# Two layers of attention and gated units on one core: half of the second layer's attention products as three f16 rounds instead of one f32 product

## The chip, the cores and the metric

The kernel runs on one core of a Trainium2 chip. The metric is the device time of one execution in microseconds, as the median of several runs. The engines are named as the profile names them: PE (TensorE) does the matrix products, ACT (ScalarE) and DVE (VectorE) the work on rows, POOL (GpSimd) the rest of it, and SP (SyncE) issues most of the DMAs.

## The reference

The computation applies the same attention block and the same gated block twice, with the same weights, to a sequence of 2048 rows of 448 numbers. There are 16 query heads of 28 numbers and one key head and one value head that all of them share.

```python
def _A_ref(x, wq, wk, wv, wo):
    q = (x @ wq).reshape(B, S, H, Dh).transpose(0, 2, 1, 3)
    k = x @ wk
    v = x @ wv
    scores = einsum("bhqd,bkd->bhqk", q, k) * (Dh ** -0.5)
    p = softmax(scores, axis=-1)
    o = einsum("bhqk,bkd->bhqd", p, v)
    return o.transpose(0, 2, 1, 3).reshape(B, S, H * Dh) @ wo

def _B_ref(x, w_gate, w_up, w_down):
    h = sigmoid(x @ w_gate) * (x @ w_up)
    return h @ w_down

x = x + _A_ref(layernorm(x), wq, wk, wv, wo)
x = x + _B_ref(layernorm(x), w_gate, w_up, w_down)
x = x + _A_ref(layernorm(x), wq, wk, wv, wo)
x = x + _B_ref(layernorm(x), w_gate, w_up, w_down)
```

## The kernel before

The kernel issues its instructions in an order written out by hand (`manual_schedule`), and each engine works through its own instructions in that order.

A layer (`l` is 0 or 1) is cut into 16 units (`u`) of 128 query rows, and a unit into 16 steps (`kt`) of 128 keys. In a step, `scores` is called four times, once for each group `g` of four heads. It makes one f16 product `s` of 128 keys by 512 (four heads times 128 rows), and ACT turns it into the probabilities `P` (128x512, f32, not yet divided by their sum) with an exponential. The scores are made in one f16 product although more than f16 precision is kept: the operand has the high part of the keys, the low part and the row maximum side by side in its 96 rows.

`pv` multiplies the values `VV` (128 keys by 32 columns: 28 values, a column of ones that gives the sum of the probabilities, and zeros) with the four `P` of a step, in f32. The four products of a step go side by side into four column tiles of 32 (`tile_position=(0, 32 * g)`) and add up over the 16 steps of a unit in one PSUM bank.

The order of work inside a step is a string in `PATHS`. A letter S is one call of `scores`, P one call of `pv` on the oldest step that waits, M one group of row maxima for a later unit (four `mx` products, then four reductions on DVE), X one tick of the work on finished units (`tile`, stages `f0` to `ff`), and F one slice of filling work (the gated block, `wo`, queries). Two strings alternate over even and odd steps. For the second layer from unit 4 they are

```python
"D0": ("FXFFSSSSPPM", "FSFSFXSFFMS"),     # even units up to 12
"D1": ("SFFXFSFSSPPM", "SFSFFFXSFSFM"),   # odd units up to 13
"E0": ("FXFFSSSSPPM", "SSFFFXSFFMS"),     # unit 14
"E1": ("SFSFXFSSFPPM", "SSSFFXSM"),       # unit 15
```

So the two P of a pair stand together in the even step: first the product of the even step before, then that of the odd step before. Between a score and its use lie a whole pair for an even step and one step for an odd one.

Work that follows a product is put off with `defer(fn, lag)`; `flush()` issues what has come due, at the start of each slice and whenever a PSUM tile is taken for filling work, and `flush(True)` issues everything that is pending, due or not. Seven PSUM banks (tag `f`) are shared by the scores, the maxima and the filling work; `P` has 14 buffers.

The stages of a finished unit that matter here: `f0` to `fw` send the sums through DRAM and back as `lb`; `fa` (step 7) multiplies on POOL (L671); `fb` (step 8) casts the result on ACT (L677) and takes the remainder on DVE (L678); `wo_products` follows, and its end starts the statistics of the layer norm with six small POOL instructions (L308 to L313); `fd` (step 14) does the norm on DVE and the remainder `hl` on POOL (L324, L325). In the gated block, `glu` leaves `ev` (DVE, L756), then `parts` (ACT, L759) with a lag of 3 and the remainder of `h` (DVE, L760) with another lag of 3.

Of the kernel before, what the change touches and what calls it, by code (L numbers as in the profile page):

```python
# [8 lines left out]
F32 = mybir.dt.float32  # L9
F16 = mybir.dt.float16  # L10
I32 = mybir.dt.int32
AF = mybir.ActivationFunctionType
OP = mybir.AluOpType
# [6 lines left out]
def interleaved_layers_kernel(ctx: ExitStack, tc: tile.TileContext, x, wq, wk, wv, wo, wg, wu, wd, out, layers=2):  # L20
# [6 lines left out]
    nc = tc.nc  # L27
    _, S, D = x.shape
    F = wg.shape[1]
    H, Dh = 16, 28  # L30
    NT, NB, G, KT, FC = S // 128, S // 512, H // 4, S // 128, F // 128
# [6 lines left out]
    cst = ctx.enter_context(tc.tile_pool(name="cst", bufs=1))  # L38
    drm = ctx.enter_context(tc.tile_pool(name="drm", bufs=1, space=DRAM))
    big = ctx.enter_context(tc.tile_pool(name="big", bufs=5))  # L40
    lay = ctx.enter_context(tc.tile_pool(name="lay", bufs=2))
    wk1 = ctx.enter_context(tc.tile_pool(name="wk1", bufs=2))
# [23 lines left out]
    def defer(fn, lag=0):  # L66

        pend.append((now[0] + lag, fn))

    def flush(every=False):  # L70
        todo, pend[:] = pend[:], []
        for i, (due, fn) in enumerate(todo):
            if due > now[0] and not every:
                pend.append((due, fn))
            else:
                fn()
        if every and pend:
            flush(True)

    def fps(shape, dt, name):  # L80
        flush()
        return psf.tile(shape, dt, tag="f", name=name, bufs=NBK["f"])
# [13 lines left out]
    pwb = cst.tile([128, 4], F32, name="pwb")  # L96
    swb = cst.tile([128, 4], F32, name="swb")
    esc = cst.tile([128, 1], F32, name="esc")
    gsc = cst.tile([128, 1], F32, name="gsc")
    osc = cst.tile([128, 1], F32, name="osc")  # L100
    dsc = cst.tile([128, 1], F32, name="dsc")
# [260 lines left out]
    for t in ktl:  # L362
        nc.vector.memset(t, 0.0)
        nc.vector.memset(t[:, 0, 28:29], 32768.0)
    KK, VV, QH = {}, {}, {}

    def layer_tiles(l):
        KK[l] = lay.tile([128, 2, S], F16, tag="KK", name="KK")
        VV[l] = lay.tile([128, KT, 32], F32, tag="VV", name="VV")
        nc.vector.memset(VV[l][:, :, 28:32], 0.0)  # L370
        nc.vector.memset(VV[l][:, :, 28:29], 1.0)

    def kv(l, XT, t, kt):

        p = fps([128, 56], F32, "kv")
        yield from chain(p, lambda a, c, k: WKV[:k, a, c], lambda c, k: XT[:k, c, t * 128:(t + 1) * 128], 40, False)
        kt_ = ktl[kt % 2]

        def build():
            k = p[:, 0:28].rearrange("p (o d) -> p o d", o=1).to_broadcast([128, 7, 28])  # L380
            nc.scalar.activation(kt_[:, 1:8, 0:28], k, AF.Copy, scale=2.0 ** -18)
            nc.scalar.activation(VV[l][:, kt, 0:28], p[:, 28:56], AF.Copy, scale=2.0 ** -16)
            nc.vector.scalar_tensor_tensor(kt_[:, 0, 0:28], p[:, 0:28], 2.0 ** -18, kt_[:, 1, 0:28],
                                           op0=OP.mult, op1=OP.subtract)
        defer(build)
# [49 lines left out]
    QS, QH, PVS = {}, {}, {}  # L435
# [147 lines left out]
    def scores(l, u, kt, g, P):  # L583
        assert ("m", l, u) in stored, (l, u, kt)
        s = psf.tile([128, 512], F32, tag=BANKS["s"], name="s", bufs=NBK[BANKS["s"]])
        nc.tensor.matmul(s, KK[l][0:96, 0, kt * 128:(kt + 1) * 128], QS[l, u][:, g].rearrange("p h n -> p (h n)"),  # L586
                         start=True, stop=True)
        p = wk1.tile([128, 512], F32, tag="P", name="P", bufs=14)
        nc.scalar.activation(p, s, AF.Exp, scale=esc)  # L589
        P.append(p)  # L590

    def pv(l, u, kt, P):
        if kt == 0:
            PVS[l, u] = psv.tile([128, 512], F32, tag="v", name="pv")
        v = PVS[l, u]
        for g in range(4):
            nc.tensor.matmul(v[32 * g:32 * g + 32], VV[l][:, kt], P[g], start=kt == 0, stop=kt == KT - 1,  # L597
                             tile_position=(0, 32 * g))
        if kt == KT - 1:
            o = wk1.tile([128, 512], F32, name="pvs", bufs=1)  # L600
            nc.scalar.copy(o, v)
            PVS[l, u] = o
# [285 lines left out]


    layer_tiles(0)  # L890
    XT0 = [big.tile([128, 7, 512], F16, tag="big", name="XT0") for _ in range(NB)]
    QH0 = wk1.tile([128, G, 512], F16, tag="wgu", name="QH0", bufs=WB)
    for b in range(NB):
        XTQ[0, b] = XT0[b]
    xr0 = {}

    def load_x0(i, eng=nc.sync):
        if i < HB:
            xr0[i] = wk1.tile([128, D], F32, tag="h", name="xr0", bufs=HB)
        else:  # L900
            xr0[i] = wk1.tile([128, D], F32, tag="P", name="xr0", bufs=14)
        eng.dma_start(xr0[i], x[0, i * 128:(i + 1) * 128])

    hl0, ls0 = {}, {}
# [126 lines left out]
    for o in SEQ.split():  # L1031
        a = o.split(",")
# [35 lines left out]
    for l in range(layers):  # L1068
# [8 lines left out]
        else:  # L1077
            mx.todo.sort()
            n = sum(a[0] < 4 for a in mx.todo) + 4
# [10 lines left out]
        for step in range(U * KT):  # L1090
            u, kt = divmod(step, KT)
            if step == HEAD and not final:
                mxs[l + 1] = Maxima(l + 1)
            P = []
            pair = pair_of(l, u)
            single = len(pair) == 2 and "P" in pair[0] and "P" in pair[1]
            for o in pair[kt % len(pair)]:
                if o == "S":
                    scores(l, u, kt, len(P), P)
                elif o == "M":  # L1100
                    if l and step < 3 * KT:
                        n = step in sparse
                    else:
                        n = 1 + (u == 0 and kt in MORE)
                    if not n:
                        mx.visit()
                    for _ in range(n):
                        if not mx.step() and not final and l + 1 in mxs:
                            a = mxs[l + 1].between()
# [24 lines left out]
        while waiting:  # L1134
            pv(*waiting.pop(0))
        flush(True)
        later(*BLK[l, NBL - 1].tile(U - 1))
        n = 0
        nx = None if final else mxs[l + 1]
        while side or pend or (fill.gens if final else not nx.started()):  # L1140
# [4 lines left out]
            a = None if final else nx.between()  # L1145
            if a:
# [7 lines left out]
                if go:  # L1154
                    nx.step(a)
                    n = 0
# [25 lines left out]
```

## Time and profile before

| | us |
|---|---|
| Median of three runs | 2247.08 (2245.97 to 2248.66) |
| Span of the profiled execution | 2242.6 |
| Busy PE / DVE / ACT / POOL in the span | 2197.5 / 1633.7 / 1556.5 / 328.6 |
| Second layer, units 4 to 15, by the copies of their sums | from 1410 to 2157 |
| An even unit / an odd unit there | 64 / 62 |

The profiled execution is not timed apart from its span; the median of the runs is 4.5 us above the span, and these 4.5 us are taken as what lies around it. A product on PE is listed with a duration that runs from its entry into the array to its end, so neighbours overlap; the distance from start to start tells what one costs. Rows of the timeline give the start, the busy time, the engine, the line, what is written and read, and how many instructions were merged into the row. The bracket at the end is the idle time before it and what ended that.

### The profile page before, as it was taken

The page shows a single profiled execution, that of the slowest core. Times are in us where ns is not written, and L with a number is a line of the kernel's source. Part 1 is how long each engine was busy: PE and PEld are TensorE (multiplying, and loading weights), DVE is VectorE, ACT ScalarE, POOL GpSimd, SP SyncE. Part 2 cuts the span into 40 slices and gives each one's busy share as a digit, 9 for nine tenths or more (in the row PEclk, how much of TensorE's full clock was granted, in tenths as well). Part 3 has the DMA queues.
Part 4 walks back from the last instruction along what each step waited for, and adds up shares of the span by engine and source line. Part 5 has one row for each costly group of instructions (what it writes and reads, how often), then busy time and mean ns, then how long its engine had stood idle before and what let it go on. Part 6 is the DMA issues. An engine that isn't in the chain of part 4 may idle for free.

```text
span 2242.6 us, 41405 instructions
## 1 busy us (share of the span) xinstructions
PE 2197.5 (98%) x15922; PEld 1032.1 (46%) x15922; DVE 1633.7 (73%) x2902; ACT 1556.5 (69%) x2603; POOL 328.6 (15%) x567
## 2 busy tenths in 40 slices
PE   7899999999999999999999999999999999999999
PEld 3322344444444444454564334445454545445457
DVE  7888887778778777777796557777777777777222
ACT  5698887777667677676514997777676767777741
POOL 4123764001110100101011010000000000000010
PEclk9999999999999999999999999999999999999999
DMA  5232662324323132422441123232231313132333
GB/s 174 70 98 87 209 211 83 105 62 118 98 67 102 58 109 61 127 78 69 135 136 40 31 56 113 52 107 80 86 101 58 107 50 104 56 107 78 97 105 118
DMA packets 203622, 213.28 MB, mean 95 GB/s; under 512 B 135376, under 2 KB 164240, under 8 KB 203424
## 3 DMA queue, kind: packets, MB, share of 16 engines
q1 hardware_dynamic: 198880, 195.88, 29.6%
q0 software_dynamic: 4544, 14.77, 1.7%
q8 instruction: 124, 2.03, 0.4%
q14 instruction: 74, 0.61, 0.1%
HBM read 175.37 MB, written 23.59 MB: 89 GB/s over the span
## 4 chain that ended last, share of the span: by engine, by line
PE 86%; DVE 4%; DMA 2%; ACT 2%; issue 1%; SPq 1%; POOL 0%; ACTq 0%; POOLq 0%; DVEq 0%
PE pv L597 20%; PE s L586 20%; PE dn L786 11%; PE gp L354 11%; PE up L354 11%; PE mx L551 7%; PE wo L697 3%; DVE mp L556 3%; PE qp L354 2%; ACT P L589 1%; DMA rc<-sums 1%; DMA sums<-rc 0%; DMA rgu<-in_B_w_gate_dram 0%; DMA lb<-sums 0%; PE hot L918 0%
## 5 line engine op out<-in xcount | busy, mean ns | idle before, releaser
L589 ACT ACTIVATE P<-s,esc 128x512 f32<-128x512 f32 x2048 | 1295.7, 692 | 455.8 <-PE s L586 444.6
L556 DVE TENSOR_REDUCE mp<-mx 128x1 f32<-128x512 f32 x2048 | 1269.6, 683 | 387.1 <-PE mx L551 382.7
L586 PE MATMUL s<-QS,KK 96*128 96x512 f16 x2048 | 687.0, 382 | 13.3 <-DVE mp L556 9.0
L354 PEld LDWEIGHTS <-wgu 128*128 128x128 f16 x4928 | 470.6, 97 | 174.6 <-issue 30.1
L597 PE MATMUL pv<-P,VV 128*32 128x512 f32 x4096 | 510.3, 602 | 0.0
L354 PE MATMUL gp<-XT,wgu 128*128 128x256 f16 x2464 | 350.3, 272 | 0.8 <-DVE mp L556 0.8
L354 PE MATMUL up<-XT,wgu 128*128 128x256 f16 x2464 | 347.7, 272 | 0.0
L786 PE MATMUL dn<-WD,h 128*128 128x448 f16 x1344 | 299.9, 352 | 0.0
L586 PEld LDWEIGHTS <-KK 96*128 96x128 f16 x2048 | 190.7, 97 | 232.6 <-issue 142.2
L597 PEld LDWEIGHTS pv<-P,VV 128*32 128x32 f32 x4096 | 98.7, 108 | 240.1 <-issue 238.9
L551 PE MATMUL mx<-KK,QH 32*128 32x512 f16 x1792 | 186.8, 384 | 5.3 <-DVE mp L556 1.9
L786 PEld LDWEIGHTS <-h 128*128 128x128 f16 x1344 | 127.1, 97 | 127.6 <-issue 11.2
L551 PEld LDWEIGHTS <-QH 32*128 32x128 f16 x1792 | 46.5, 91 | 247.8 <-issue 245.4
L671 POOL TENSOR_TENSOR lb<-pvs,lb 128x512 f32<-128x512 f32 x32 | 41.2, 1287 | 622.3 <-DMA lb<-sums 548.7
L759 ACT ACTIVATE h<-th 128x512 f16<-128x512 f32 x112 | 70.4, 628 | 67.4 <-DVE th L756 67.3
L308 POOL TENSOR_SCALAR rs<-mv 128x1 f32<-128x1 f32 (+1 forms) x50 | 12.2, 244 | 678.0 <-DVE mv L293 676.0
L354 PE MATMUL qp<-XT,WQ 128*128 128x512 f16 x352 | 109.5, 389 | 1.0 <-DVE mp L556 0.7
L756 DVE SCALAR_TENSOR_TENSOR th<-th,up 128x512 f32<-128x512 f32 x112 | 76.2, 680 | 42.2 <-PE up L354 36.7
L748 ACT ACTIVATE th<-gp,gsc 128x512 f32<-128x512 f32 x112 | 76.8, 686 | 32.3 <-PE gp L354 32.2
L760 DVE SCALAR_TENSOR_TENSOR h<-th,h 128x512 f16<-128x512 f32 x112 | 77.0, 688 | 29.6 <-ACT h L759 29.6
L697 PE MATMUL wo<-WO,oT 128*128 128x448 f16 x384 | 88.8, 352 | 0.9 <-ACT oT L677 0.5
L354 PEld LDWEIGHTS <-WQ 128*128 128x128 f16 x352 | 33.6, 99 | 49.7 <-issue 23.1
(158 smaller groups left out, 908.2 us busy)
## 6 DMA issues: line engine op xcount, KB each, us to landing
wgu<-wgu_d SPq DMA_DIRECT2D x224, 512.0 KB
QS<-qd SPq DMA_DIRECT2D x384, 32.0 KB
lb<-sums SPq DMA_DIRECT2D x128, 64.0 KB
xr<-in_A_x_dram SPq DMA_DIRECT2D x32, 224.0 KB
qd<-qst POOLq DMA_DIRECT2D x28, 256.0 KB, 2.6
wgu_d<-sgu POOLq DMA_DIRECT2D x14, 512.0 KB, 4.0
x2d<-x SPq DMA_DIRECT2D x16, 224.0 KB
xr<-x2d SPq DMA_DIRECT2D x16, 224.0 KB
```

The lines of the kernel that those rows point to most:

```text
L354: nc.tensor.matmul(ps, a, b, start=n == 0, stop=n == 10)
L551: nc.tensor.matmul(ps[h][:, i * w:(i + 1) * w], qh[32 * h:32 * h + 32, g], KK[l][32 * h:32 * h + 32, 1, ka:kz], start=True, stop=True, til ...
L556: nc.vector.tensor_reduce(o, ps[h].rearrange("p (g k) -> p g k", g=n), axis=AX.X, op=OP.max)
L586: nc.tensor.matmul(s, KK[l][0:96, 0, kt * 128:(kt + 1) * 128], QS[l, u][:, g].rearrange("p h n -> p (h n)"), start=True, stop=True)
L589: nc.scalar.activation(p, s, AF.Exp, scale=esc)
L597: nc.tensor.matmul(v[32 * g:32 * g + 32], VV[l][:, kt], P[g], start=kt == 0, stop=kt == KT - 1, tile_position=(0, 32 * g))
L697: nc.tensor.matmul(p, v["oT"][:, a, h * 128:(h + 1) * 128], WO[:, c, h], start=n == 0, stop=n == 11)
L748: defer(lambda: nc.scalar.activation(th, gp.rearrange("p j n -> p (j n)"), AF.Tanh, scale=gsc))
L756: nc.vector.scalar_tensor_tensor(t, th, 1.0, up.rearrange("p j n -> p (j n)"), op0=OP.add, op1=OP.mult)
L759: nc.scalar.activation(h[:, 0], t, AF.Copy, scale=2.0 ** -17)
L760: defer(lambda: nc.vector.scalar_tensor_tensor(h[:, 1], t, 2.0 ** -17, h[:, 0], op0=OP.mult, op1=OP.subtract), 3)
L786: nc.tensor.matmul(p, hs[f // 2][:, a, o:o + 128], WD[:, f, c], start=n == 0, stop=n == 3 * FC - 1)
```

## The change

In the second layer the exponential gets a bias of 4 ln 2, which multiplies every probability and their sums by 16. From unit 4 of that layer on, the probabilities of every even step are split: a high part `hi` in f16 (a copy, by DVE for groups 0 and 2 and by ACT for groups 1 and 3) and a remainder `lo` in f16 (a subtraction on POOL). The split is put off with a lag of 3 slices. The values are split in the same way into `VH`, on POOL, when they are made. `pv` of such a step is then twelve f16 products in three rounds of four column tiles, high by high, low values by high, high values by low, after a `flush(True)`. The parts lie three groups to a tile in the pool `big`. `P` has 13 buffers instead of 14.

```diff
+    up4 = cst.tile([128, 1], F32, name="up4")
+    nc.vector.memset(up4, 4 * math.log(2))
...
     def layer_tiles(l):
...
+        if l:
+            VH[l] = lay.tile([128, KT, 2, 32], F16, tag="VH", name="VH", bufs=1)
...
             nc.scalar.activation(VV[l][:, kt, 0:28], p[:, 28:56], AF.Copy, scale=2.0 ** -16)
+            if l in VH:
+                nc.gpsimd.tensor_copy(VH[l][:, kt, 0], VV[l][:, kt])
+                nc.gpsimd.tensor_tensor(VH[l][:, kt, 1], VV[l][:, kt], VH[l][:, kt, 0], op=OP.subtract)
...
-        p = wk1.tile([128, 512], F32, tag="P", name="P", bufs=14)
-        nc.scalar.activation(p, s, AF.Exp, scale=esc)
-        P.append(p)
+        p = wk1.tile([128, 512], F32, tag="P", name="P", bufs=13)
+        nc.scalar.activation(p, s, AF.Exp, scale=esc, bias=up4 if l else 0.0)
+        if not halved(l, u, kt):
+            P.append(p)
+            return
+        if not hold or hold[1] == 3:
+            hold[:] = [big.tile([128, 7, 512], F16, tag="big", name="PH"), 0]
+        t, n = hold
+        hold[1] += 1
+        hi, lo = t[:, 2 * n], t[:, 2 * n + 1]
+        P.append((hi, lo))
+        how = HI[g]
+
+        def part():
+            if how == "a":
+                nc.scalar.copy(hi, p)
+            else:
+                (nc.vector if how == "d" else nc.gpsimd).tensor_copy(hi, p)
+            nc.gpsimd.tensor_tensor(lo, p, hi, op=OP.subtract)
+        defer(part, HLAG)
+
+    hold = []
+    HI, HLAG = "dada", 3
+
+    def halved(l, u, k):
+        return l and u > 3 and k % 2 == 0
 
     def pv(l, u, kt, P):
...
         v = PVS[l, u]
-        for g in range(4):
-            nc.tensor.matmul(v[32 * g:32 * g + 32], VV[l][:, kt], P[g], start=kt == 0, stop=kt == KT - 1,
-                             tile_position=(0, 32 * g))
+        if halved(l, u, kt):
+            flush(True)
+            for n, (a, c) in enumerate(((0, 0), (1, 0), (0, 1))):
+                for g in range(4):
+                    nc.tensor.matmul(v[32 * g:32 * g + 32], VH[l][:, kt, a], P[g][c],
+                                     start=kt == 0 and n == 0, stop=kt == KT - 1 and n == 2,
+                                     tile_position=(0, 32 * g))
+        else:
+            for g in range(4):
+                nc.tensor.matmul(v[32 * g:32 * g + 32], VV[l][:, kt], P[g], start=kt == 0, stop=kt == KT - 1,
+                                 tile_position=(0, 32 * g))
...
-            xr0[i] = wk1.tile([128, D], F32, tag="P", name="xr0", bufs=14)
+            xr0[i] = wk1.tile([128, D], F32, tag="P", name="xr0", bufs=13)
```

More of the change, by code (lines that the diff above doesn't have):

```diff
@@ L364, in interleaved_layers_kernel @@
         nc.vector.memset(t[:, 0, 28:29], 32768.0)
-    KK, VV, QH = {}, {}, {}
+    KK, VV, VH, QH = {}, {}, {}, {}
     def layer_tiles(l):
```

## The prediction

> **What bounds the kernel now.** I read the page first, then the busy times by unit, the waits of the second layer, and the timeline of one even and one odd unit.
>
> ```profile
> span 2242.6 us, 41405 instructions
> PE 2197.5 (98%) x15922; PEld 1032.1 (46%) x15922; DVE 1633.7 (73%) x2902; ACT 1556.5 (69%) x2603; POOL 328.6 (15%) x567
> 1663.00:1727.00 64.00, 64.00 (x452) 28.89 (x448) 47.47 (x81) 44.57 (x71) 4.01 (x9) 1.00 0.20 58
> 1727.00:1789.00 62.00, 61.65 (x482) 31.57 (x478) 48.73 (x83) 46.40 (x75) 4.01 (x9) 1.00 0.40 110
> 2105.00:2157.00 52.00, 52.00 (x393) 28.32 (x392) 8.78 (x15) 40.66 (x70) 4.03 (x9) 1.00 0.38 119
> ACT P L589 <- PE s L586: 162.7, 232, 1.5
> DVE mp L556 <- PE mx L551: 126.4, 127, 2.2
> PE s L586 <- DVE mp L556: 0.6, 2, 0.3
> ```
>
> The three long rows are unit 8 (even), unit 9 (odd) and unit 15: length, then busy PE, weight loads, DVE, ACT, POOL, and the granted clock (1.00). The last three are waits between 1474 and 2105 us (units 5 to 14). PE is never idle there, and the others wait for it: ACT 163 us of 631 for scores, DVE 126 us for maxima, PE only 0.6 us for DVE. So a shorter product shortens these units, as long as what is added to ACT, DVE and POOL fits where they wait.
>
> **The product.** One even and one odd unit, a pair of steps each, PE first, then ACT, then DVE:
>
> ```profile
> 1699.23 1.05 PE L586 MATMUL s<-QS,KK 96*128 96x512 f16 x4
> 1700.21 1.92 PE L597 MATMUL pv<-P,VV 128*32 128x512 f32 x16
> 1702.06 0.39 PE L551 MATMUL mx<-KK,QH 32*128 32x512 f16 x4
> 1708.45 1.92 PE L597 MATMUL pv<-P,VV 128*32 128x512 f32 x16
> 1716.99 1.85 PE pv L597 x16
> ...
> 1706.18 0.69 ACT L589 ACTIVATE P<-s,esc 128x512 f32<-128x512 f32 x1 [0.85 <-PE s L586]
> 1707.91 2.42 ACT L589 ACTIVATE P<-s,esc 128x512 f32<-128x512 f32 x4 [1.04 <-PE s L586]
> 1711.67 0.69 ACT L589 ACTIVATE P<-s,esc 128x512 f32<-128x512 f32 x1 [1.33 <-PE s L586]
> ...
> 1705.85 2.48 DVE L556 TENSOR_REDUCE mp<-mx 128x1 f32<-128x512 f32 x4 [0.88 <-PE mx L551]
> 1710.77 1.89 DVE L556 TENSOR_REDUCE mp<-mx 128x1 f32<-128x512 f32 x3
> ...
> 1764.17 1.92 PE L597 MATMUL pv<-P,VV 128*32 128x512 f32 x16
> 1771.36 1.06 PE L597 MATMUL pv<-P,VV 128*32 128x512 f32 x8
> 1763.90 1.84 ACT L589 ACTIVATE P<-s,esc 128x512 f32<-128x512 f32 x3 [0.73 <-PE s L586]
> 1766.78 2.63 ACT L589 ACTIVATE P<-s,esc 128x512 f32<-128x512 f32 x4 [1.03 <-PE s L586]
> 1762.16 2.48 DVE L556 TENSOR_REDUCE mp<-mx 128x1 f32<-128x512 f32 x4 [0.78 <-PE mx L551]
> 1766.45 2.48 DVE L556 TENSOR_REDUCE mp<-mx 128x1 f32<-128x512 f32 x4 [0.34 <-PE mx L551]
> ```
>
> Two `pv` take 1702.06 - 1700.21 = 1.85 us from start to start, one 0.93: sixteen products are four rounds of four column tiles, 0.46 each, two to a step, because an f32 product is listed as two. Four f16 products of 512 columns in a row (1699.23) start (1.05 - 0.38) / 3 = 0.22 apart, 0.38 being the duration of one. If four column tiles run beside each other in f16 as they do in f32, a round costs 0.22, three 0.66, and a halved step saves 0.27 us. There are 12 units x 8 = 96 of them: 25.9 us, the whole the change can give.
>
> The low end of that price comes from the only packed f16 product, the four `mx`, whose successor starts 0.32 later:
>
> ```profile
> 1603.53 0.40 PE L551 MATMUL mx<-KK,QH 32*128 32x512 f16 x4
> 1603.85 0.39 PE L586 MATMUL s<-QS,KK 96*128 96x512 f16 x1
> 1605.81 0.16 PEld L597 LDWEIGHTS pv<-P,VV 128*32 128x32 f32 x8 [0.42 <-issue]
> 1606.27 0.13 PEld L597 LDWEIGHTS pv<-P,VV 128*32 128x32 f32 x4 [0.30 <-issue]
> ```
>
> Three times 0.32 is 0.96, dearer than f32 by 0.03. I take 0.22: the 0.32 holds a change of tiling on leaving, which inside three equal rounds does not occur, and eight weight loads stand at the start of the f32 rounds, so those of the second round are loaded ahead. Four loads take 0.13, which fits under 0.21.
>
> The Trainium skill (TensorE: Matmul & The Clock Gate, Part 3, what overlaps) says that a weight load runs under a product only if its row group differs. All four column tiles here use all rows, so by that rule the loads would stand open. The loads at 1605.81 go against it. By that rule a round would be 0.22 + 0.13 = 0.35, three 1.05, and the kernel slower by 96 x 0.12 = 11.5 us, to 2259.
>
> **What is added.** Four groups per pair, with durations from the group rows:
>
> ```profile
> L323 DVE CAST hl<-xn 128x448 f16<-128x448 f32 x10 | 3.9, 394 | 0.3
> L677 ACT CAST oT<-lb 128x512 f16<-128x512 f32 x10 | 6.1, 607 | 0.0
> L143 POOL TENSOR_TENSOR sgu<-rgu,sgu 128x512 f16<-128x512 f32 x9 | 10.4, 1160 | 0.7
> L760 DVE SCALAR_TENSOR_TENSOR h<-th,h 128x512 f16<-128x512 f32 x35 | 23.6, 674 | 0.0
> 230.30 1.16 POOL L143 TENSOR_TENSOR sgu<-rgu,sgu 128x512 f16<-128x512 f32 x1
> 230.39 1.62 DVE L131 SCALAR_TENSOR_TENSOR sgu<-rgu,swb,sgu 128x512 f16<-128x512 f32 x1
> ```
>
> DVE: two copies of 0.394 x 512 / 448 = 0.45, so 0.90. ACT: two of 0.61, so 1.22. POOL: four of 1.16, and about 0.09 between them (estimate), so 5.0 of a pair of about 8 us. POOL was idle for 60 of 64 us.
>
> Where they fall: `part` has a lag of 3 slices, but each halved `pv` calls `flush(True)` and so issues the parts of its own step at once, just ahead of the two `pv`. In unit 8 that is 1708.45. Exponentials end there at 1708.5, 1709.1, 1709.7, 1710.3. Between 1708.33 and 1710.77 DVE has nothing but, once a unit, a row maximum (two `pv` make this gap in every pair), so it copies group 0 at once; POOL's first remainder runs to about 1710.3. The copy of group 2 is ready at 1709.8 and meets it.
>
> The last two rows show what then happens: a DVE instruction that reads two tiles in SBUF began 0.09 after a POOL subtraction, ended when that had ended plus 0.55, and was listed with 1.62, where a like one (L760) takes 0.67. So the second copy waits about 0.5 and ends at 1710.75; the next maxima, which a shorter `pv` brings to about 1710.5, are delayed by 0.25, and the gap of 0.88 ahead of the following ones takes that up.
>
> The Trainium skill (SBUF — State Buffer, on the pair of ports shared by VectorE and GpSimd) says the same: one holds the pair for a whole instruction, the other blocks fully, and copies and casts can be of the holding kind. By that rule every copy may lose 1.16 to a remainder; rival three prices this.
>
> ACT's two copies follow the exponentials at 1710.33 and end at 1711.6, in the gap of 1.33. The remainders of groups 1 to 3 follow, the last ending near 1714.8, 6.3 after the `pv` that issued it. It is needed in the third round of the next pair, 1716.99 + 0.44: 2.6 us to spare. So even units keep the whole: 6 x 8 x 0.27 = 13.0 us.
>
> An odd unit has less room. DVE is idle 62 - 48.73 = 13.3 us. Copies take 8 x 0.90 = 7.2, waits of the second copy 8 x 0.5 = 4.0, and the remainders of `h`, four in such a unit, meet a busy POOL (8 x 4.64 / 62 = 0.6 of the time) for half an instruction: 4 x 0.6 x 0.58 = 1.4. That leaves 0.7 of the 2.2 us wanted; I take 0.5: 5 x 0.5 = 2.5 us. In unit 15 ACT is idle 52 - 40.66 = 11.3, and 16 x 0.61 = 9.8 leaves 1.5; I take 1.0.
>
> Losses. POOL's two jobs for a finished unit now stand in line:
>
> ```profile
> 1747.81 1.27 POOL L671 TENSOR_TENSOR lb<-pvs,lb 128x512 f32<-128x512 f32 x1 [28.90 <-DMA lb<-sums]
> 1755.65 0.61 ACT L677 CAST oT<-lb 128x512 f16<-128x512 f32 x1
> 1766.20 0.22 POOL L308 TENSOR_SCALAR rs<-mv 128x1 f32<-128x1 f32 x1 [17.12 <-DVE mv L293]
> 1767.98 0.19 POOL L313 TENSOR_TENSOR rs<-rs 128x1 f32<-128x1 f32 x1
> 2150.63 1.92 PE L597 MATMUL pv<-P,VV 128*32 128x512 f32 x16
> 2154.77 1.92 PE L597 MATMUL pv<-P,VV 128*32 128x512 f32 x16
> ```
>
> The product `lb` runs 6.6 us ahead of the ACT cast that needs it. Behind four remainders it would end some 7 us later than now, so the cast, with the exponentials behind it, starts about 0.6 late; half is absorbed by ACT's gaps: 5 x 0.3 = 1.5 us in odd units, nothing in even ones with their longer steps. The six `rs` instructions hold POOL for 2.0 us, between the first and second remainder of a pair: in unit 9 the last remainder then ends near 1772.4 and is wanted at 1771.36 + 0.44; 0.6 x 5 = 3.0 us. In unit 4 the first halved step has no halved `pv` beside it and waits its lag: 1 us (estimate). At the end the last halved `pv` (2154.77) comes 4.1 after the one that issues its parts; the remainder needs 6.3, the third round is at 4.6: 1.7 us.
>
> At nothing: the 32 small POOL instructions for `VH` (POOL idles), the bias (ACT's input beside the scale, same shape), and the thirteenth buffer (twelve `P` are in flight at most when two `pv` release eight, and the scores of the fourteenth stand behind these `pv` on PE anyway). The early issue of pending work by `flush(True)` brings ACT's `h` and its DVE remainder forward into the same gap; the work is the same, so zero, between -3 and +5.
>
> Sum: 13.0 + 2.5 + 1.0 - 1.5 - 3.0 - 1.0 - 1.7 = 9.3 us. The span goes to 2233.3, and with the 4.5 us around it the time to 2238.
>
> **Rivals.** *All of it is kept* (odd units hide the additions too): 25.9 - 2.7 for the two single losses, 2224. For it: waits of DVE for maxima are 126 us in ten units, copies need 72. Against it: the 0.34 left ahead of the maxima at 1766.45.
>
> *The product does not get shorter*: a round costs 0.32, nothing is saved, and the losses of 7 us stand partly in the shadow: 2247, from 2243 to 2255.
>
> *The shared reads decide against it* (slower): both DVE copies of a pair wait for a remainder, 1.62 - 0.67 = 0.95 each. An odd pair then needs 48.73 / 8 + 0.90 + 1.9 = 8.9 on DVE instead of 7.75, an even one 47.47 / 8 + 2.8 = 8.7 instead of 8.0. Then 40 odd pairs give +46 and 40 even ones +28: 2321 at worst. With one full wait per pair it is 7.95 against 7.75 in odd pairs, +8, and even ones still fit: about 2245. It decides from about 0.75 us of waiting per odd pair, where DVE has no idle time left; halfway, 2275. For it: the 1.62. Against it: at the time of the first copy POOL has been through for 2 us.
>
> **How the numbers follow.** This measurement can tell about 0.2% (4.5 us) from no change. Chances: forecast (2230 to 2243) 0.44, all kept (2221 to 2230) 0.18, no shorter product 0.16, shared reads 0.17 (2250 to 2321), loads that stand open 0.05. Below 2242.6: 0.44 + 0.18, less 0.01 for the forecast's edge, 0.61; within: this 0.01, 0.13 of the third and 0.02 of the fourth, 0.16; above 2251.6: the other 0.03, 0.15 and 0.05, 0.23. The range reaches from 2222 to 2262; what is left out is the top of the second case (0.04) and the worse half of the fourth (0.12). The likeliest case alone is 2230 to 2243.
>
> **What would show it.** Halved `pv` as twelve f16 products in about 0.66 us; DVE casts at 0.45 for group 0 and near 1 for group 2; remainders at 1.16; even units near 62 us, odd ones near 61.5; PE's idle time in units 5 to 14 a few us and ended by POOL. Rounds 0.3 apart, DVE busy over 95% of an odd unit, or waits of PE for POOL in every pair would make it wrong.

## Result and profile after

The changed kernel takes 2278.8 us (median of four, 2276.8 to 2280.4) against 2247.9: a ratio of 1.014 (95% interval 1.0126 to 1.0155), slower by 31 us. 2238 had been forecast, with a range up to 2262.

The page of the changed kernel: span, busy times, then groups (line, engine, what is written and read, count, busy us, mean ns, idle before):

```profile
span 2276.6 us, 43034 instructions
PE 2200.2 (97%) x16306; PEld 1043.5 (46%) x16306; DVE 1739.7 (76%) x3095; ACT 1724.7 (76%) x2795; POOL 787.4 (35%) x983
L596 ACT ACTIVATE P<-s,esc 128x512 f32<-128x512 f32 x1024 | 650.2, 691 | 235.0 <-PE s L593 228.9
L596 ACT ACTIVATE P<-s,up,esc 128x512 f32<-128x512 f32 x1024 | 729.6, 800 | 86.0 <-PE s L593 80.0
L613 POOL TENSOR_TENSOR PH<-P,PH 128x512 f16<-128x512 f32 x384 | 448.0, 1190 | 218.1 <-DVE PH L612 150.7
L612 DVE CAST PH<-P 128x512 f16<-128x512 f32 x192 | 102.2, 541 | 67.1 <-ACT P L596 66.7
L798 DVE SCALAR_TENSOR_TENSOR h<-th,h 128x512 f16<-128x512 f32 x112 | 93.0, 830 | 22.6 <-ACT h L797 22.3
```

PE is as busy as before; ACT has 168 us more, DVE 106, POOL 459. The second row of L596 is the exponential of the second layer, with the bias: 800 ns instead of 691, 1024 times. The remainder of `h` (L798, two inputs in SBUF) went from 688 (L760 before) to 830 ns in the mean of all 112.

Units 8, 9 and 15 by engine (columns as before), then the waits from 1480 to 2150 us, about units 5 to 14:

```profile
1683.80:1748.40 64.60, 63.12 (x478) 28.88 (x477) 54.63 (x98) 56.50 (x88) 40.84 (x42) 1.00 0.19 57
1748.40:1813.50 65.10, 62.06 (x518) 32.77 (x517) 58.54 (x100) 59.23 (x92) 42.47 (x42) 1.00 0.34 105
2136.50:2190.80 54.30, 51.32 (x423) 28.66 (x421) 20.88 (x30) 53.04 (x85) 40.39 (x40) 1.00 0.36 116
```

```profile
ACT P L596 <- PE s L593: 57.7, 102, 1.0
DVE mp L563 <- PE mx L558: 29.3, 47, 1.0
PE s L593 <- DVE mp L563: 5.4, 9, 0.8
```

An even unit takes 64.6 us (64 before), an odd one 65.1 (62), unit 15 54.3 (52). Before, ACT and DVE spent 163 and 126 us waiting for PE; now 58 and 29. In an odd unit ACT is busy for 59.2 of 65.1 us and DVE for 58.5, and PE, idle for 1.7 us in all of units 5 to 14 before, is idle for 21.7. None of the three is full by its busy time.

One pair of `pv` in unit 8 on PE, the weight loads of the halved one, and the exponentials beside it:

```profile
1712.89 0.83 PE L630 MATMUL pv<-PH,VH 128*32 128x512 f16 x12
1713.55 1.03 PE L635 MATMUL pv<-P,VV 128*32 128x512 f32 x8
1714.51 0.39 PE L558 MATMUL mx<-KK,QH 32*128 32x512 f16 x3
1712.89 0.34 PEld L630 LDWEIGHTS <-VH 128*32 128x32 f16 x12 [0.42 <-issue]
1713.58 2.77 ACT L596 ACTIVATE P<-s,up,esc 128x512 f32<-128x512 f32 x4
```

The halved `pv` costs 1713.55 - 1712.89 = 0.66 us, as forecast. But the f32 `pv` behind it costs 1714.51 - 1713.55 = 0.96, not 0.93. The pair takes 1.62 us instead of 1.85, so a halved step saves 0.23 us and not 0.27. Four exponentials take 2.77 us where they took 2.42. In an odd unit, DVE, POOL and PE right after a halved `pv`:

```profile
1762.60 0.68 DVE L794 SCALAR_TENSOR_TENSOR th<-th,up 128x512 f32<-128x512 f32 x1
1763.20 1.01 DVE L612 CAST PH<-P 128x512 f16<-128x512 f32 x1
1764.14 1.63 DVE L798 SCALAR_TENSOR_TENSOR h<-th,h 128x512 f16<-128x512 f32 x1
1765.70 4.93 DVE L563 TENSOR_REDUCE mp<-mx 128x1 f32<-128x512 f32 x8
1762.77 5.13 POOL L613 TENSOR_TENSOR PH<-P,PH 128x512 f16<-128x512 f32 x4 [3.50 <-DVE PH L612]
1766.43 0.38 PE L593 MATMUL s<-QS,KK 96*128 96x512 f16 x1 [0.83 <-DVE mp L563]
```

POOL starts four remainders at 1762.77. `flush(True)` has issued, with the copies, everything pending of the gated block (L794, L798). The second copy takes 1.01 us where the first took 0.42, the remainder of `h` 1.63 instead of 0.68, and the maxima, whose products ended at about 1763.7, are reduced only from 1765.70. They hold four banks, and PE waits 0.83 us for one.

The comparison below uses two numbers of each kernel: the median time, and the length of units 4 to 15 in its profile, from the copy of the sums (`pvs`) that ends unit 3 to the one that ends unit 15 (746.9 us before, 767.2 in the changed kernel). The second leaves out what varies earlier: in the nine kernels with 13 buffers that are the same up to unit 4 the copy that ends unit 3 came anywhere between 1410.0 and 1414.4 us. It is one execution, though, and the median is several. The kernel before was timed again beside each group of kernels and took 2244.3 to 2247.9 us, so where kernels of different groups are compared, each is taken by its distance from the kernel before of its own group.

### The profile page after: what moved, and what is told of

The parts are those of the page before. It is cut to its first block, busy times and chain, and to the rows that moved or that the text cites. A ratio compares the mean times of both kernels' runs of the same rounds, so it can differ in the third digit from the quotient of the medians.

```text
span 2276.6 us, 43034 instructions
## 1 busy us (share of the span) xinstructions
PE 2200.2 (97%) x16306; PEld 1043.5 (46%) x16306; DVE 1739.7 (76%) x3095; ACT 1724.7 (76%) x2795; POOL 787.4 (35%) x983
## 5 line engine op out<-in xcount | busy, mean ns | idle before, releaser
L596 ACT ACTIVATE P<-s,esc 128x512 f32<-128x512 f32 x1024 | 650.2, 691 | 235.0 <-PE s L593 228.9
L596 ACT ACTIVATE P<-s,up,esc 128x512 f32<-128x512 f32 x1024 | 729.6, 800 | 86.0 <-PE s L593 80.0
L613 POOL TENSOR_TENSOR PH<-P,PH 128x512 f16<-128x512 f32 x384 | 448.0, 1190 | 218.1 <-DVE PH L612 150.7
L635 PE MATMUL pv<-P,VV 128*32 128x512 f32 x3328 | 424.9, 600 | 0.0
L558 PE MATMUL mx<-KK,QH 32*128 32x512 f16 x1792 | 195.2, 386 | 7.9 <-ACT P L596 4.5
L635 PEld LDWEIGHTS pv<-P,VV 128*32 128x32 f32 x3328 | 83.0, 109 | 164.3 <-issue 140.6
L612 DVE CAST PH<-P 128x512 f16<-128x512 f32 x192 | 102.2, 541 | 67.1 <-ACT P L596 66.7
L610 ACT CAST PH<-P 128x512 f16<-128x512 f32 x192 | 110.9, 634 | 0.0
L798 DVE SCALAR_TENSOR_TENSOR h<-th,h 128x512 f16<-128x512 f32 x112 | 93.0, 830 | 22.6 <-ACT h L797 22.3
```

The lines of the kernel that those rows point to most:

```text
L558: nc.tensor.matmul(ps[h][:, i * w:(i + 1) * w], qh[32 * h:32 * h + 32, g], KK[l][32 * h:32 * h + 32, 1, ka:kz], start=True, stop=True, til ...
L596: nc.scalar.activation(p, s, AF.Exp, scale=esc, bias=up4 if l else 0.0)
L610: nc.scalar.copy(hi, p)
L612: (nc.vector if how == "d" else nc.gpsimd).tensor_copy(hi, p)
L613: nc.gpsimd.tensor_tensor(lo, p, hi, op=OP.subtract)
L798: defer(lambda: nc.vector.scalar_tensor_tensor(h[:, 1], t, 2.0 ** -17, h[:, 0], op0=OP.mult, op1=OP.subtract), 3)
```

## Experiments

The theory: the bias makes ACT dearer and, with the copies, a second bottleneck. The rival: POOL's reads shut DVE out.

**Bias alone** in the kernel before:

```diff
-        nc.scalar.activation(p, s, AF.Exp, scale=esc)
+        nc.scalar.activation(p, s, AF.Exp, scale=esc, bias=up4 if l else 0.0)
```

> The kernel before, with nothing of the change but the bias of 4 ln 2 in the exponentials of the second layer. Theory one (the bias costs ACT time: in the changed kernel four exponentials in a row take 2.79 us busy where they took 2.42): units 0 to 3, where ACT is the bound, lose the 13.5 us that they lost in the changed kernel, units 4 to 15 have 19 us of idle ACT per unit against 64 x 0.09 = 6 and lose 0 to 4: 2261 to 2265. Rival (units 0 to 3 lose for another reason, such as 13 buffers for P, and the bias is free as I had predicted): 2246 to 2250.

Measured: 2257.9 (ratio 1.0057, 1.0045 to 1.007), +12.5 us. Units 1 to 3 took 154.2 us instead of 147.3, units 4 to 15 749.8 instead of 746.9. Nearly all of the loss in units 1 to 3 is in units 1 and 2 (3.5 and 2.7 us), where ACT was busy for 39.5 of 42.2 and 40.9 of 43.7 us before. The bias is not free; theory one holds, slightly below its range.

**Without the bias**, the rest of the change as it is:

```diff
-        nc.scalar.activation(p, s, AF.Exp, scale=esc, bias=up4 if l else 0.0)
+        nc.scalar.activation(p, s, AF.Exp, scale=esc)
```

> The changed kernel without the bias; the probabilities are split unscaled. Theory one (the bias takes 96 x 4 x 2 x 0.09 us of ACT, which with the copies has no room left): units 0 to 3 come back by 13.5 us and units 4 to 15 fall from 767 to between 732 and 747: 2232 to 2246. Rival (VectorE and GpSimd shut each other out, and that holds units 4 to 15): only the 13.5 us come back, 2263 to 2267.

Measured: 2260.3 (1.0068, 1.0055 to 1.0082); units 4 to 15 758.1 us. That is 15.0 us above the kernel before of its group, where the changed kernel was 31.0 above its own. So the bias cost 16 of the 31 us, 9.2 of these in units 4 to 15, where alone it had cost 3. But 15 us stay: between the two expectations. Both theories had a part. Units 8 and 9 of this kernel:

```profile
1672.40:1735.50 63.10, 62.64 (x481) 29.00 (x479) 56.87 (x98) 51.69 (x88) 40.92 (x42) 1.00 0.21 58
1735.50:1801.70 66.20, 62.24 (x518) 32.55 (x517) 59.76 (x100) 54.43 (x93) 42.59 (x42) 1.00 0.33 103
```

The even unit gains a little (63.1), the odd one loses 4.

**The products alone**: f16 written by the exponential at once, no copies, no remainders.

```diff
+        hi = t[:, 2 * n]
+        nc.scalar.activation(hi, s, AF.Exp, scale=esc)
+        P.append((hi, hi))
```

> The changed kernel without the bias and without the split: of an even step the exponential writes f16 at once, and the remainder's round uses the high part again (no copies on ACT and DVE, no remainders on POOL; the products of these steps are not those of the reference). It keeps the three rounds on PE and the order of issue, so it gives the saving on PE alone. If a halved step is 0.27 us shorter and nothing else stands in the way: 2247.5 - 25.9 = 2221 to 2223. If something else in the order (the early issue of pending work, one P buffer less) eats it: above 2230. Both theories expect the first.

Measured: 2230.1 (0.9929, 0.9917 to 0.9942); units 4 to 15 730.3, 16.6 us less than before. Not 25.9, which both theories had expected; the time lies at the edge of the second case, that something else eats part of the saving. The starts of PE's rows in units 5 to 14 show two parts of it. The `pv` products took 128.7 us where they had taken 147.4, which is 0.23 for each of 80 halved steps, as in the pair above. And everything else on PE took 5.3 us more.

**Copies, but no remainders**:

```diff
-            nc.gpsimd.tensor_tensor(lo, p, hi, op=OP.subtract)
-        P.append((hi, lo))
+        P.append((hi, hi))
```

> The changed kernel without the bias and without the 384 remainders on POOL; the copies on ACT and DVE stay, and the third round uses the high part (not the reference's products). Against the one without the bias alone it gives what POOL costs. Theory one: at most 8 us less than that kernel, 2225 to 2238. Rival (shut out by POOL): 20 us or more less than that kernel, 2225 to 2245 while that one stays at 2265.

Measured: 2231.4 (0.9941, 0.9928 to 0.9955), units 4 to 15 733.4. The 384 remainders cost 29 us (24.7 in units 4 to 15), the 384 copies 1 to 3. The rival is right. Even units are 62.0 now, 2.1 less than before, but odd ones 62.1, as before. DVE's two groups from 1480 to 2130 us, without remainders (this kernel) and with them (the one without the bias):

```profile
L612 DVE CAST PH<-P 128x512 f16<-128x512 f32 x170 | 75.1, 455 | 33.6 <-ACT P L596 33.3
L797 DVE SCALAR_TENSOR_TENSOR h<-th,h 128x512 f16<-128x512 f32 x37 | 25.4, 686 | 7.9 <-ACT h L796 7.8
```

```profile
L612 DVE CAST PH<-P 128x512 f16<-128x512 f32 x162 | 101.7, 638 | 31.3 <-ACT P L596 31.3
L798 DVE SCALAR_TENSOR_TENSOR h<-th,h 128x512 f16<-128x512 f32 x35 | 37.7, 1078 | 0.1
```

A copy goes from 455 to 638 ns, a remainder of `h` from 686 to 1078, beside a POOL that reads SBUF: with 160 copies and 35 remainders 43 us over ten units.

The next four take the kernel without the bias apart.

**Only the parts issued early.** `part` goes to a list of its own, and a halved `pv` empties that list instead of calling `flush(True)`:

```diff
-        defer(part, HLAG)
+        own.append((now[0] + HLAG, part))
...
-            flush(True)
+            while own:
+                own.pop(0)[1]()
```

> The changed kernel without the bias (2260 us), and a halved pv issues only the parts of the split that are pending, not everything that is pending; the rest of the pending work (h of the gated block and its remainder on VectorE) keeps its lag. Theory one (in odd units the early issue puts the remainder of h right behind the second copy, where GpSimd blocks it: 1.08 us in the mean instead of 0.69, and the maxima start late): odd units lose 1 to 3 us less, 2245 to 2254. Rival (VectorE meets a busy GpSimd wherever the work is put): 2257 to 2263.

Measured: 2245.8 (1.0001, 0.9992 to 1.0009), 14.8 us less; units 4 to 15 746.4, odd ones 62.6 to 63.2. Theory one's time, at the edge of its range, but not for its reason: the remainder of `h` is as blocked as before, 1108 ns in the mean (the rows stand further below) against 1078. What changed is what stands behind it. The same pair of unit 9 on DVE (and PE's wait), first with everything issued at once, then with the parts alone:

```profile
1766.66 1.65 DVE L798 SCALAR_TENSOR_TENSOR h<-th,h 128x512 f16<-128x512 f32 x1
1768.23 1.38 DVE L612 CAST PH<-P 128x512 f16<-128x512 f32 x1
1769.53 1.87 DVE L563 TENSOR_REDUCE mp<-mx 128x1 f32<-128x512 f32 x3
1770.26 0.60 PE L356 MATMUL up<-XT,wgu 128*128 128x256 f16 x4 [1.53 <-DVE mp L563]
```

```profile
1760.29 1.39 DVE L614 CAST PH<-P 128x512 f16<-128x512 f32 x1
1761.59 2.47 DVE L565 TENSOR_REDUCE mp<-mx 128x1 f32<-128x512 f32 x4
1763.99 1.47 DVE L801 SCALAR_TENSOR_TENSOR h<-th,h 128x512 f16<-128x512 f32 x1
```

In the first the maxima stand behind a blocked copy and a blocked remainder, and PE waits 1.53 us for a bank. In the second the remainder is blocked too (1.47), but behind the maxima, and PE does not wait. PE's idle time in units 5 to 14 falls from 19.9 to 7.7 us.

**One copy on DVE**:

```diff
-    HI, HLAG = "dada", 3
+    HI, HLAG = "daaa", 3
```

> The changed kernel without the bias, with the copy of group 2 on ScalarE instead of VectorE: VectorE copies only group 0, when GpSimd is done with the pair before, so no copy is blocked. Theory one (blocked VectorE is what holds the odd units): VectorE is freed of 8 x 0.64 = 5 us per unit, 2244 to 2254. Rival (all engines are near full, and ScalarE, at 54 of 65 us in odd units, takes 5 us more): 2258 to 2270.

Measured: 2257.0 (1.0054, 1.0041 to 1.0066): 3.5 us less, nearer to the rival. The copies on DVE are unblocked (419 ns), and odd units gain 1.2 us for it (64.3), but even ones lose 0.8 (63.9) and unit 15 loses 1.9 (52.3), with a third copy on ACT.

**P not held by POOL**, `lo = hi - hi`:

```diff
-            nc.gpsimd.tensor_tensor(lo, p, hi, op=OP.subtract)
+            nc.gpsimd.tensor_tensor(lo, hi, hi, op=OP.subtract)
```

> The changed kernel without the bias, with the remainder computed as high part minus high part (zero, so the low round adds nothing: not the reference's products). GpSimd has the same 384 subtractions at the same places and with two reads in SBUF, but P is free once it is copied. Theory one (GpSimd's reads block VectorE): 2255 to 2262. Rival (thirteen buffers of P are held longer by the late remainders, and the exponentials wait for them: 6.8 us of such waits in units 5 to 14): 2240 to 2252.

Measured: 2252.2 (1.0029, 1.0018 to 1.004), 8 us less, at the upper edge of the rival's range. POOL's remainders are also shorter here, so the hold of `P` is not yet told apart from their length.

**Only even units halved**:

```diff
-        return l and u > 3 and k % 2 == 0
+        return l and u > 3 and u % 2 == 0 and k % 2 == 0
```

> The changed kernel without the bias, halving only in even units (4, 6, .. 14). From the lengths of units without the bias (even 63.0 against 64.2 before, odd 65.3 against 61.9): five odd units come back by 3.4 us each, unit 15 gives up its 1.5: 2260 - 17 + 1.5 = 2243 to 2247. If the loss in odd units is handed on from the even ones, it stays above 2252.

Measured: 2252.8 (1.0031, 1.0019 to 1.0042). A miss: the time is that of the second case, but its reason is not, since odd units came back to 61.7 to 62.9, while even ones went to 65.1. In an even unit the halved `pv` of the unit before, which would issue its first parts, is missing; they wait for their lag, and PE waits for POOL once in each of these units, 0.9 us. That is about what an even unit lost against the 64.1 before; why the saving of its halved steps does not show was not looked into.

With the parts alone, two kernels asked for a cheaper dose, one for a cheaper place, one for the floor.

**Every fourth step**, the list of the parts emptied at each `pv`, halved or not, and the same **with four copies on ACT** (the lines of `HI` in the second alone):

```diff
-        return l and u > 3 and k % 2 == 0
+        return l and u > 3 and k % 4 == 0
...
-        if halved(l, u, kt):
-            while own:
-                own.pop(0)[1]()
+        while own:
+            own.pop(0)[1]()
+        if halved(l, u, kt):
...
-    HI, HLAG = "dada", 3
+    HI, HLAG = "aaaa", 3
```

> No bias, a list of their own for the parts of the split, issued at the first pv of the same step, and only every fourth step halved: 48 instead of 96. If the saving is 0.27 us a step and the cost of the remainders shrinks faster than their number, since VectorE then has idle time left for blocked instructions: 2245.5 - 13 + 3 for the slower first layer + 1 to 4 for blocks: 2236 to 2240. Rival (cost in proportion to the number, as gain and cost cancel at 96): 2243 to 2248.

> As the one with every fourth step halved, with all four copies on ScalarE: VectorE gets nothing from the change but blocks of the remainder of h. If blocked copies are what is left of the cost: 1 to 3 us below that kernel, 2233 to 2238. Rival (four copies in a row, 2.5 us, hold the exponentials of the next step, and the scores wait for banks): 2240 to 2250.

Measured: 2243.9 (0.9996, 0.9987 to 1.0004) and 2250.2 (1.0031, 1.0019 to 1.0043); units 4 to 15 744.3 and 749.9. Both rivals by their times, the second at its upper edge. The first agrees with gain and cost in proportion to the number, but as they cancel, it does not show either by itself. In the second PE waits 5.0 us for ACT in units 5 to 14, and not at all in the first.

**Parts alone, one copy on DVE** (the list emptied at each `pv` here too), and **parts alone, no remainders**:

```diff
-    HI, HLAG = "dada", 3
+    HI, HLAG = "daaa", 3
```

```diff
-            nc.gpsimd.tensor_tensor(lo, p, hi, op=OP.subtract)
...
-        P.append((hi, lo))
+        P.append((hi, hi))
```

> The kernel whose pv issues only the parts (2245.7 us, 96 halved steps), with one copy on VectorE and three on ScalarE. If the block of the second copy (0.61 us in the mean for the two, 0.45 without GpSimd) is what takes up the gain there: 2238 to 2243. Rival (ScalarE has no room for a third copy: with one in the other kernel even units went from 63.0 to 64): 2248 to 2256.

> The kernel whose pv issues only the parts (2245.7 us), without the remainders on GpSimd (the third round uses the high part; not the reference's products). Against the kernel without remainders that issues everything pending (2231.4): if the early issue hurts only because GpSimd then blocks what is issued, 2228 to 2233. If it hurts by itself: 2215 to 2222.

Measured: 2245.2 (1.0003, 0.9994 to 1.0011), neither expectation; and 2227.5 (0.9926, 0.9914 to 0.9938), units 4 to 15 727.3, just below the first expectation. So the early issue costs 3.2 us without remainders and 14.8 with them (6.1 and 11.7 in units 4 to 15): the larger part of it comes through POOL, not all. The remainders cost 17.4 us even with the parts alone (19.1 in units 4 to 15).

What these 17 us consist of was open. **Copies 1 and 2 on DVE**, the same **with 14 buffers** (made room for by the values of the halved steps alone and one buffer for `mr`), and **parts alone with `lo = hi - hi`** (the edit is the one above, on top of the parts alone):

```diff
-    HI, HLAG = "dada", 3
+    HI, HLAG = "adda", 3
...
-        p = wk1.tile([128, 512], F32, tag="P", name="P", bufs=13)
+        p = wk1.tile([128, 512], F32, tag="P", name="P", bufs=14)
...
-            VH[l] = lay.tile([128, KT, 2, 32], F16, tag="VH", name="VH", bufs=1)
+            VH[l] = lay.tile([128, KT // 2, 2, 32], F16, tag="VH", name="VH", bufs=1)
...
-        r = wk1.tile([16, 128], F16, name="mr")
+        r = wk1.tile([16, 128], F16, name="mr", bufs=1)
```

> The kernel whose pv issues only the parts (2245.7 us), with the copies of groups 0 and 3 on ScalarE and those of 1 and 2 on VectorE. ScalarE's first copy stands behind all four exponentials, so GpSimd begins when VectorE has nearly done both of its copies: the same work on every engine, but no blocked copy (0.61 us in the mean there, 0.45 unblocked). If blocked copies are the larger part of the 18 us: 2233 to 2240. If not: 2243 to 2248; and GpSimd begins later, so a pv that waits for the last remainder would show.

> As the one before, with 14 buffers of P again (room for it: VH holds only even steps, and the row of maxima has one buffer). If held buffers take part: 2 to 6 us below the one before. If they do not: the same within 2 us.

> The kernel whose pv issues only the parts (2245.7 us), the remainder computed as high minus high, so that GpSimd does not hold P (1.07 instead of 1.19 us each; not the reference's products). With everything issued at once this brought 8 us (2260.3 to 2252.2). If the hold of P is the cause: 2236 to 2240. If blocked VectorE is: 2243 to 2246, the shorter remainders giving 1 to 2.

Measured: 2251.3 (1.0038, 1.0015 to 1.006), 2247.9 (1.0015, 1.0006 to 1.0024), 2235.7 (0.996, 0.9947 to 0.9974); units 4 to 15 754.4, 750.0, 734.7. The profiled execution of the first had a lower granted clock (0.95) up to 1668 us, which takes in units 4 to 7, so its 754.4 is too long; in units 8 to 15, at 1.00, it takes 496.0 us, 3.7 more than with `dada`. Blocked copies are not the larger part: with fewer of them (535 ns in the mean instead of 607) the time rose. POOL then waits for ACT's copy behind four exponentials (160.6 us of its idle time from 1480 to 2130 us end with that copy); that this is why was not shown. The fourteenth buffer brought 3.4 us (1.3 in units 8 to 15), so held buffers may take a small part in this order. The third, 9 us less (11.7 in units 4 to 15), spoke for the hold.

**Parts alone with 14 buffers**, **the first two copies on DVE** with 14, and **15 buffers** (room by one buffer for `qst`); the lines of the buffers are as above:

```diff
-    HI, HLAG = "dada", 3
+    HI, HLAG = "ddaa", 3
...
-        q = wk1.tile([128, 2, 512], F16, name="qst")
+        q = wk1.tile([128, 2, 512], F16, name="qst", bufs=1)
```

> No bias, the pv issues only the parts, copies as in the change, 14 buffers of P (VH holds only even steps, the row of maxima has one buffer). If held buffers make up the 10 us between 2245.7 and 2235.7: about half of it, 2238 to 2243. If the length of the remainders does: 2244 to 2247.

> As the one before, with the copies of groups 0 and 1 on VectorE and of 2 and 3 on ScalarE: the first two remainders start right behind their exponentials and the last ends about 0.5 us earlier, at the price of one copy that is always blocked. Hold: 0 to 3 us below the one before. Blocked copies: 1 to 4 us above it.

> As the first of these, with 15 buffers of P (one buffer less for the queries' tile qst, which could cost up to 2 us before unit 4). Hold: all of the 10 us and perhaps 1 more, 2234 to 2240. Length of the remainders: 2243 to 2248.

Measured: 2245.8 (1.0, 0.9991 to 1.0009), 2239.2 (0.9969, 0.9957 to 0.9981), 2251.3 (1.0024, 1.0014 to 1.0035); units 4 to 15 746.5, 738.4, 745.9. In the order `dada` the buffers do nothing (746.4, 746.5 and 745.9 with 13, 14 and 15), so the hold is not the cause of the 9 us (the third kernel's loss lies before unit 3 ends, at 1418.8 us instead of 1409.9). The order `ddaa` brings 8.1 us in units 4 to 15 against `dada`, 6.6 in the median, more than either theory had said, and gives the one version with the full remainders (but, as all here, without the bias) that is faster than the kernel before, by 0.3%. DVE with `dada` and 13 buffers, then with `ddaa`, 1480 to 2130 us, and one pair of the latter on DVE and POOL:

```profile
L614 DVE CAST PH<-P 128x512 f16<-128x512 f32 x166 | 98.6, 607 | 30.2 <-ACT P L598 30.0
L801 DVE SCALAR_TENSOR_TENSOR h<-th,h 128x512 f16<-128x512 f32 x36 | 39.9, 1108 | 0.1
```

```profile
L612 DVE CAST PH<-P 128x512 f16<-128x512 f32 x168 | 86.5, 542 | 17.4 <-ACT P L596 12.9 <-POOL PH L613 4.3
L799 DVE SCALAR_TENSOR_TENSOR h<-th,h 128x512 f16<-128x512 f32 x36 | 29.5, 819 | 0.0
```

```profile
1757.10 0.69 DVE L717 TENSOR_TENSOR oT<-lb,oT 128x512 f16<-128x512 f32 x1
1757.70 1.38 DVE L612 CAST PH<-P 128x512 f16<-128x512 f32 x1
1759.01 2.47 DVE L563 TENSOR_REDUCE mp<-mx 128x1 f32<-128x512 f32 x4
1761.40 0.68 DVE L799 SCALAR_TENSOR_TENSOR h<-th,h 128x512 f16<-128x512 f32 x1
1757.27 1.54 POOL L613 TENSOR_TENSOR PH<-P,PH 128x512 f16<-128x512 f32 x1 [1.44 <-DVE PH L612]
1759.16 2.27 POOL L613 TENSOR_TENSOR PH<-P,PH 128x512 f16<-128x512 f32 x2 [0.36 <-DVE PH L612]
1761.39 1.70 POOL L613 TENSOR_TENSOR PH<-P,PH 128x512 f16<-128x512 f32 x1
```

The block goes both ways: POOL's first remainder begins at 1757.27 under a DVE instruction with two inputs in SBUF (1757.10 to 1757.79) and takes 1.54 instead of 1.16; DVE's copy, issued under it, takes 1.38 instead of 0.42. The four maxima at 1759.01, which read PSUM, run beside POOL in 2.47 us, as before (2.48). The remainder of `h` begins at 1761.40, where one POOL subtraction has ended, and passes in 0.68; the next subtraction takes 1.70 in its place. In the mean the remainder of `h` takes 819 ns instead of 1108. The expectation had one copy of each pair always blocked, but the mean of the copies fell too, to 542 ns: 29 of 168 begin under a POOL subtraction, 47 of 166 with `dada`.

The Trainium skill (SBUF — State Buffer, who interferes with whom) says that whoever starts first has the shared pair for the whole instruction. The rows agree, in both directions.

## Why the prediction was wrong

The forecast was 9.3 us less, the measurement 31.0 more. The experiments divide this difference step by step, each against the kernel before of its group: the products and copies, with the parts alone issued early, bring 17.2 us; the remainders cost 17.4, which leaves +0.2; the early issue of everything else costs 14.8, which makes +15.0; the bias costs 16.0, which makes +31.0. The prediction had the last two at nothing. Without them it would have been 9.5 us off, by the product's size and by the losses.

*The product*: the 0.66 us were right, the saving was mis-sized. The prediction took half of a pair of `pv` (0.93) as the price of either, but the f32 one that stays costs 0.96 behind an f16 one, so 96 halved steps save about 22.5 us and not 25.9. And of what `pv` saves, the rest of PE's work takes part or all back. From the starts of PE's rows in units 5 to 14:

| | `pv`, us | all else on PE, us |
|---|---|---|
| Before | 147.4 | 483.5 |
| Parts alone, no remainders | 128.7 | 485.4 |
| The products alone, everything issued | 128.7 | 488.8 |
| Copies, no remainders, everything issued | 128.7 | 491.1 |
| Parts alone, `ddaa`, 14 buffers | 128.8 | 493.3 |
| Parts alone | 128.7 | 501.9 |
| Without the bias | 128.7 | 513.5 |
| Changed kernel | 128.7 | 518.0 |

The rule of the Trainium skill on row groups (TensorE: Matmul & The Clock Gate, Part 3) does not show here: twelve products with twelve loads (0.34 us in all) pass in 0.66, so loads of the next column tiles do not stand open.

*"At nothing: ... the bias"*: the first step that failed. Four exponentials take 2.77 instead of 2.42 us, 0.09 each. Alone that is 12.5 us, and in the changed kernel 16. The argument "ACT's input beside the scale, same shape" was not looked up in a row, and no row of the profile before had an exponential with such an operand.

The Trainium skill (ScalarE: Activation LUTs, what ACT_TABLE_LOAD costs) states the price: each [128,1] pointer operand adds about 93 ns to an ACTIVATE. The 0.09 agree. An estimate by it, 1024 x 0.093 = 95 us of ACT work, would have shown the term.

*"The early issue ... zero, between -3 and +5"*: the second step that failed. It costs 3.2 us without remainders and 14.8 with them. "The work is the same" is true, but the place decides what waits behind it: the remainder of `h`, blocked by POOL in either place, stands ahead of the maxima that PE waits for.

*The blocks*: the sizes were about right, their effect was not. Forecast were 0.5 us per second copy and 0.35 per remainder of `h`; measured (everything issued, no bias) 0.18 per copy, 0.37 per pair, and 0.39. But I took DVE's remaining idle time as usable ("that leaves 0.7 of the 2.2 us wanted"). Odd units lost about 3 us, with and without the bias, with DVE and ACT at 82 to 91% busy. This idle time stood between dependent steps of engines that work in order, and was no reserve.

*Even units keep the whole 13 us*: without the bias units 6 to 14 kept 1.1 us each of the 2.15 forecast, and unit 4 lost 1.4; with it none kept anything.

*POOL's jobs in line*: the cast that waits for `lb` was 0.9 us late in the six even units 4 to 14, and on time in the odd ones, where 0.6 had been forecast. The stall behind the `rs` instructions did not show; in units 5 to 14 PE waits for none of POOL's remainders. The two single waits came as forecast: 0.6 us in unit 4 (1 forecast), 1.4 at the end (1.7).

*VH and the thirteenth buffer at nothing*: right. In the nine kernels with both but no bias units 1 to 3 take 147.2 to 147.3 us, as before (147.3), and later a fourteenth buffer does nothing in the order of the change.

*Rival three* (shared reads, chance 0.17) had the sign and part of the cause, DVE held up by the shared reads. That the time fell into its range is luck in part: 16 of the 31 us are the bias, which it did not have, and a pair lost 0.37 us by blocked copies, where it decided "from about 0.75".

None of the three signs that were to make the forecast wrong came: rounds are 0.22 apart, DVE is busy for 90% of an odd unit, and PE waits for POOL in no pair of units 5 to 14. They looked at POOL and at full engines; PE waited for DVE's maxima.

DVE's copies and remainders of `h` without the remainders, then POOL's remainders with the full ones and with `lo = hi - hi`, all with the parts alone, 1480 to 2130 us:

```profile
L614 DVE CAST PH<-P 128x512 f16<-128x512 f32 x171 | 77.6, 465 | 41.5 <-ACT P L598 41.1
L800 DVE SCALAR_TENSOR_TENSOR h<-th,h 128x512 f16<-128x512 f32 x37 | 25.1, 677 | 3.5 <-ACT h L799 3.4
```

```profile
L615 POOL TENSOR_TENSOR PH<-P,PH 128x512 f16<-128x512 f32 x334 | 389.7, 1190 | 173.7 <-DVE PH L614 161.2 <-ACT PH L612 10.9 <-PE s L595 0.6
```

```profile
L615 POOL TENSOR_TENSOR PH<-PH 128x512 f16<-128x512 f16 x339 | 353.8, 1067 | 202.1 <-DVE PH L614 171.4 <-ACT PH L612 17.9 <-PE pv L633 11.7
```

What stays open: how the 17 us of the remainders divide. DVE's blocked time differs by 36 us between the kernels with and without them (98.6 + 39.9 against 77.6 + 25.1 us, parts alone), but with `lo = hi - hi` the copies are nearly as blocked (601 ns in the mean) and the time is 9 us less. Its remainders are 1067 instead of 1190 ns, and its `h` 870 instead of 1108; which of these counts was not taken apart.

## What to carry to other kernels

Price every operand, not every instruction: an added per-partition operand cost 0.09 us, and 1024 times that was half of the loss. Before work goes to a free engine, look at whom its SBUF reads shut out, and at what waits behind the blocked instruction; a call that issues "everything pending" moves other work into that place too. In these kernels maxima that read PSUM ran beside POOL undisturbed, so they are what to put there (only the orders shown were tried). Where three engines fed each other in order through a few banks here, 82 to 91% busy was full.

## What the runs showed of the hardware beyond that

Three rounds of four column-tiled f16 products of 512 columns take 0.66 us; one such set in f32 takes 0.93 as half of a pair and 0.96 behind the f16 rounds. A DVE copy of 128x512 f32 to f16 takes 0.42 us alone and, in the pair shown, 1.38 under a running POOL subtraction. With the parts alone, a row maximum of 128x512 from PSUM takes 681 ns where it begins under a POOL subtraction and 678 elsewhere, in the mean.
